# One core, a decode step over a cached K and V: 65 small loads added to the load queue

## The chip, the cores and the metric

The kernel runs on one core of a Trainium2 chip. Its engines are TensorE (PE, matrix products), VectorE (DVE), ScalarE (ACT), GpSimd (POOL) and SyncE (SP). Each runs its own program and waits for the others on semaphores. Data comes from the chip's memory (HBM) into the on-chip buffer of 128 partitions by DMA: an engine, here SP alone, issues a load, and 16 DMA engines carry it out. The metric is the device time of one execution in microseconds (us).

## What is computed

One token for each of two batch rows. x is normalized, projected to 32 heads, and each head attends over 8192 cached keys and values of 128 elements; the result is projected by wo and multiplied by a gate, which is an MLP of the same normalized x. All is 32-bit float.

```python
def ref(x, k_cache, v_cache, wq, wo, w1, b1, w2, b2):   # B=2, H=32, Sk=8192, Dh=128, D=512, F=1376
    xn = layernorm(x)
    q = (xn @ wq).reshape(B, 1, H, Dh).transpose(0, 2, 1, 3)
    scores = einsum("bhqd,bhkd->bhqk", q, k_cache) * Dh ** -0.5
    o = einsum("bhqk,bhkd->bhqd", softmax(scores), v_cache)
    s = o.transpose(0, 2, 1, 3).reshape(B, 1, H * Dh) @ wo
    h = gelu(layernorm(xn) @ w1 + b1) @ w2 + b2
    return x + s * silu(h)
```

## The kernel before

K and V are 256 MB each and are read once. The work is cut into N = 32 iterations, each for one batch row and two heads (U = 2): the K of the two heads lies in one buffer of 128 partitions, 64 for each head, 128 keys of 128 elements in a partition, 64 KB a partition and 8 MB in all. The V of an iteration has the same shape. There are three such buffers: `kb[0]` and `kb[1]` for K in turn, `vb` for V. wq is loaded into `kb[0]` before any K, the small weights w1 and w2 and the values of the MLP lie in `vb` before any V, and wo goes into `vb` after the last V but one. The last V goes into `kb[1]`, in two halves.

In an iteration, DVE multiplies the K buffer by the query in place (`scores_mul`, L524, two halves) and sums over the 128 elements (`scores_sum`, L531). PE and DVE find the largest score (L535 to L541), ACT takes the exponentials (L552), and PE multiplies them with V (`weighted`, L575, 64 matmuls). ACT, PE and DVE then fold that product into a small table Z (L582 to L590). After the last iteration come the division by the sums, the product with wo, in pieces as these land (L650, L659), two DVE operations with the gate (L668, L669), and the store of the result (L670).

All loads go through `load` (L313), which adds one DMA issue to SP's program; SP holds nothing else but waits. A small planner, `Plan`, is told for each operation what it reads and writes, finds which earlier operations it has to wait for, and `emit` writes each engine's program in the order in which the operations were added. Thus SP issues in this order: w1, x, w2, b1, b2, wq, the first K (`load_k(0)`, two halves), the second K (it waits until PE has used wq), the first V, then in turn a K (when DVE has summed the K two before) and a V (when PE has multiplied the V before), the last V, and wo in six pieces (`WO_PIECES`; the last head column in parts of 192 KB and 64 KB). Each load raises a semaphore of the name it is given, by 16 when it is complete; loads on one semaphore are counted together. At the end SP issues the store and waits for it (L125).

PE, DVE and ACT run iterations in a hardware loop; SP's program is written out.

Of the kernel before, what the change touches and what calls it, by code (L numbers as in the profile page):

```python
# [21 lines left out]
class Plan:  # L22
# [18 lines left out]
    def op(self, eng, fn, r=(), w=(), over=(), it=None, loop=False, dma=None):  # L41


        o = Op()
        o.eng, o.fn, o.it, o.loop, o.dma, o.tell = eng, fn, it, loop, dma, False
        need = {}

        def after(d, war):
            if d.dma is None and dma is None and d.eng == eng and (eng == "pe" or war):
                return  # L50
            if d.dma is None:
                if need.get(d.eng) is None or need[d.eng].idx < d.idx:
                    need[d.eng] = d
            else:
                k = ("dma", d.dma)
                if need.get(k) is None or need[k].idx < d.idx:
                    need[k] = d

        for k in r:
            if k in self.writer:  # L60
                after(self.writer[k], False)
        for k in list(w) + list(over):
            if k in self.writer:
                after(self.writer[k], False)
            for d in self.readers.get(k, ()):
                after(d, True)
        clock = self.clock[eng]
        need = {k: d for k, d in need.items() if clock.get(k, 0) < d.idx}
        o.deps = [(k, d) for k, d in need.items()
                  if not any(e is not d and e.done.get(k, 0) >= d.idx for e in need.values())]  # L70
        for _, d in o.deps:
            for k, v in d.done.items():
                clock[k] = max(clock.get(k, 0), v)
        own = eng if dma is None else ("dma", dma)
        self.count[own] = o.idx = self.count.get(own, 0) + 1
        o.done = dict(clock)
        o.done[own] = o.idx
        for k in w:
            self.writer[k] = o
            self.readers[k] = []  # L80
        for k in r:
            if k not in w:
                self.readers.setdefault(k, []).append(o)
        self.ops.append(o)

    def emit(self, heads):

        nc = self.nc
        for o in self.ops:
            for _, d in o.deps:  # L90
                d.tell = True
        sems, value, told = {}, {}, {}
        for o in self.ops:
            key = o.eng if o.dma is None else ("dma", o.dma)
            if key not in sems:
                sems[key] = nc.alloc_semaphore(o.eng if o.dma is None else f"dma_{o.dma}")

            step = 16 if o.dma is not None else int(o.tell or o.eng != "pe")
            told[key] = told.get(key, 0) + step
            value[id(o)] = told[key]  # L100
        for o in self.ops:
            o.waits = {k: value[id(d)] for k, d in o.deps}

        def put(o, waits, turn=None):
            e = self.eng[o.eng]
            for k, v in waits:
                e.wait_ge(sems[k], v)
            i = o.fn() if o.it is None else o.fn(o.it if turn is None else turn)
            if o.dma is not None:
                i.then_inc(sems[("dma", o.dma)], 16)  # L110
            elif o.tell or o.eng != "pe":
                i.then_inc(sems[o.eng], 1)

        def order(d):
            return sorted(d.items(), key=lambda kv: str(kv[0]))

        for e in self.eng:
            ops = [o for o in self.ops if o.eng == e]
            inside = [j for j, o in enumerate(ops) if o.loop]
            if not inside:  # L120
                for o in ops:
                    put(o, order(o.waits))
                if e == "sp":

                    nc.sync.wait_ge(sems[("dma", "out")], told[("dma", "out")])  # L125
                continue
            for o in ops[:inside[0]]:
                put(o, order(o.waits))
            turns = {}
            for j in inside:  # L130
                turns.setdefault(ops[j].it, []).append(ops[j])
            n, m = len(turns), len(turns[1])
            assert inside == list(range(inside[0], inside[-1] + 1)) and list(turns) == list(range(1, n + 1))
            assert all(len(t) == m for t in turns.values())


            body, ahead = [], {}
            for j in range(m):
                col = [turns[i][j] for i in range(1, n + 1)]
                assert len({o.tell for o in col[1:-1]}) == 1, j  # L140
                for o in col:
                    o.tell = col[1].tell
                ws = []
                for k in sorted(set().union(*(o.waits for o in col)), key=str):
                    if all(k not in o.waits for o in col[1:]):
                        ahead[k] = max(ahead.get(k, 0), col[0].waits[k])
                        continue
                    step = col[2].waits[k] - col[1].waits[k]
                    base = col[1].waits[k] - 2 * step
                    for o in col:  # L150
                        assert o.waits.get(k) == step * o.it + base or (o.it == 1 and k not in o.waits), \
                            (e, j, k, o.it, [x.waits.get(k) for x in col])
                    ws.append((k, step, base))
                body.append((col[1], ws))
            for k, v in order(ahead):
                self.eng[e].wait_ge(sems[k], v)
            et = self.eng[e].engine
            with nc.Fori(1, n + 1, 1, engines=bass.OrderedEngineSet([et]), head_slot={et: heads[e]}) as i:
                for o, ws in body:
                    put(o, [(k, i * step + base if base else i * step) for k, step, base in ws], i)  # L160
            for o in ops[inside[-1] + 1:]:
                put(o, order(o.waits))


def decode_kernel(nc, x, kc, vc, wq, wo, w1, b1, w2, b2, out):
    P = 128
# [44 lines left out]
    def sbuf(name, shape):  # L211
        return nc.alloc_sbuf_tensor(name, shape, F32).ap()
# [41 lines left out]
    q_nat = O4  # L254
    rl = sbuf("rl", [P, B])
    on = sbuf("on", [P, RM, OC])


    used = [0]
# [53 lines left out]
    def load(dst, src, sem, w, over=()):  # L313
        op("sp", lambda: nc.sync.dma_start(dst, src), (), w, over=over, dma=sem)  # L314

    def load_k(n):
        i = (n + 1) % 2
        if n in (0, N - 1):
            for s in range(2):
                load(kbuf[i][:, s * M:(s + 1) * M], kf[n][:, s * M:(s + 1) * M], f"k{i}{s}", [("kb", i, s)])  # L320
            return
        load(kbuf[i], kf[n], f"kb{i}", [("kb", i, s) for s in range(2)])
# [10 lines left out]
    for t, src, k in ((b1_sb, b1, "b1"), (b2_sb, b2, "b2")):  # L333
        load(t.rearrange("o (k e) -> o k e", k=16), src.rearrange("(o k e) -> o k e", o=1, k=16), k, [k])
    load(wq_sb, wq.rearrange("(p c) n -> p c n", p=P), "wq", [("kb", 0, s) for s in range(2)])
    load_k(0)


    dve(lambda: nc.vector.memset(eps_t, EPS), w=["eps"])
# [148 lines left out]
    for k in range(N // NB):  # L488

        b, e = divmod(k, HH // NB)  # L490
        i, g = divmod(e, GQ)
# [8 lines left out]

    PT, PM, PN = (t for t in scratch[:3])
    load_k(1)

    def load_v(n):
        load(vbuf, vf[n], "v", ["vb"], over=boot)

    load_v(0)

    def cols(t, a, n):

        return t[:, a:a + n] if isinstance(a, int) else t[:, bass.ds(a, n)]
# [3 lines left out]
    def vector(n, m, fn, r, w):  # L515

        o, e = n % 2, m - n
        dve(lambda i: fn(i * 2 + (e - o)), r, w, it=(n + 1) // 2, loop=0 < n < N - 1)
# [21 lines left out]
    def max_dve(n):  # L540
        vector(n + 1, n, lambda n: nc.vector.tensor_reduce(  # L541
            out=NM, in_=PM[:1, :P].rearrange("o (s r) -> o s r", s=U), axis=AX.X, op=ALU.max, negate=True),
            ["s1"], ["nm"])
# [78 lines left out]
    for i, (a, e) in enumerate(((0, CUT), (CUT, D)), len(WO_PIECES) - 2):  # L622
        load(wo_sb[:, OC - 1, a:e], wo_r[:, OC - 1, a:e], f"wo{i}", [("wo", i)], over=["vb"])

    max_dve(N - 1)
    exps(N - 1)
    weighted(N - 1)
# [72 lines left out]
```

## Time and profile before

| | |
|---|---|
| time, median of 2 runs | 1299.55 us (1299.54 to 1299.55) |
| the profiled execution's own time | 1299.38 us |
| its span, first to last instruction | 1298.1 us |
| busy: DVE, PE, ACT | 1134.3, 408.2, 77.8 us |
| read from HBM | 559.30 MB |

The profile is one execution on the chip, seen by a hardware profiler. Line numbers are those of the kernel. `vb<-in_A_v_cache_dram` is an operation that writes the tile vb from the tensor of the V cache. An engine's name with a q, as in SPq, is its instruction queue, where DMAs are issued. The chain of waits is followed back from the last instruction: at each step to what released it, or to the instruction before it on its engine. The windows view sums, for a stretch of time, each engine's busy time (with the number of instructions), the clock granted to PE, the busy share of the 16 DMA engines and the rate of what they carried; packets are counted where they start, so that over a short stretch the share can pass 1.

### The profile page before, as it was taken

The numbers are of one execution on the slowest core, as the hardware profiler recorded it, in microseconds if no ns is written. First come the engines' busy times: TensorE is split into PE (matmuls) and PEld (weight loads), VectorE is DVE, ScalarE is ACT, GpSimd is POOL, SyncE is SP. The second block draws the span as 40 slices with busy tenths as digits, with TensorE's granted clock in tenths as the row PEclk, the third lists the DMA queues.
The fourth block names the chain that finished last, engine by engine and source line by source line (L and its number), as shares of the span: only waits on it lengthen the run. The fifth ranks groups of instructions, "written<-read, shape, count | busy, mean of one in ns | idle before, by whom it ended". The sixth has DMA issues, their size and how long they took to land.

```text
span 1298.1 us, 6789 instructions
## 1 busy us (share of the span) xinstructions
PE 408.2 (31%) x2728; PEld 123.5 (10%) x2728; DVE 1134.3 (87%) x276; ACT 77.8 (6%) x250; POOL 1.4 (0%) x8
## 2 busy tenths in 40 slices
PE   5603333312333311333321333321333321233337
PEld 1100111000101100101100101000101100001102
DVE  2499999988889988889988888988888988888991
ACT  1200000000000000000000000000000000000000
POOL 0000000000000000000000000000000000000000
PEclk9856666556666556666655666655666655666659
DMA  9999999999999999999999999999999999999998
GB/s 402 449 423 444 428 434 432 426 444 428 436 432 424 446 426 444 428 432 434 426 444 428 434 434 424 446 426 444 426 428 440 426 444 428 434 434 424 433 435 363
DMA packets 11087, 559.45 MB, mean 431 GB/s; under 512 B 1236, under 2 KB 1604, under 8 KB 1736
## 3 DMA queue, kind: packets, MB, share of 16 engines
q1 hardware_dynamic: 11080, 559.36, 99.7%
q8 instruction: 4, 0.07, 0.0%
q14 instruction: 3, 0.02, 0.0%
HBM read 559.30 MB, written 0.06 MB: 431 GB/s over the span
## 4 chain that ended last, share of the span: by engine, by line
DMA 70%; PE 25%; DVE 3%; issue 1%; ACT 0%; SPq 0%; DVEq 0%
DMA vb<-in_A_v_cache_dram 67%; PE po L575 22%; DMA vb<-in_A_wo_dram 2%; DVE kb L524 1%; DVE sc L531 1%; PE s L410 1%; DMA vb<-in_A_x_dram 1%; PE po L482 1%; PE s L452 0%; PE s L412 0%; PE acc L659 0%; DVE vb L418 0%; ACT L431 0%; PE s L459 0%; SPq L314 0%
## 5 line engine op out<-in xcount | busy, mean ns | idle before, releaser
L524 DVE TENSOR_TENSOR kb<-kb,Q 128x8192 f32<-128x8192 f32 x64 | 555.5, 8681 | 102.8 <-DMA kb<-in_A_k_cache_dram 93.5
L531 DVE TENSOR_REDUCE sc<-kb 128x64 f32<-128x8192 f32 x64 | 552.3, 8666 | 0.0
L575 PE MATMUL po<-vb,PZ 128*8 128x512 f32 x1984 | 287.2, 744 | 287.3 <-DMA vb<-in_A_v_cache_dram 286.1
L547 PE MATMUL s<-nm,srow 1*128 1x2 f32 x64 | 18.4, 355 | 361.6 <-DVE nm L541 361.6
L575 PEld LDWEIGHTS po<-vb,PZ 128*8 128x8 f32 x1984 | 57.2, 104 | 491.2 <-issue 487.2
L538 PE MATMUL s<-ident,mx 128*1 128x128 f32 x32 | 11.8, 369 | 191.7 <-DVE mx L535 191.7
L547 PEld LDWEIGHTS s<-nm,srow 1*128 1x128 f32 x64 | 15.7, 302 | 370.9 <-DVE nm L541 370.9
L582 ACT COPY o<-po 128x512 f32<-128x512 f32 x32 | 18.8, 586 | 533.6 <-PE po L575 533.6
L548 ACT COPY bias<-s 128x2 f32<-128x2 f32 x32 | 5.1, 161 | 618.3 <-PE s L547 618.3
L584 PE MATMUL s<-mod,o 128*128 128x2 f32 x256 | 33.6, 253 | 22.1 <-ACT o L582 22.1
L584 PEld LDWEIGHTS s<-mod,o 128*128 128x128 f32 x256 | 31.0, 191 | 51.4 <-ACT o L582 51.4
L552 ACT ACTIVATE PZ<-sc,bias 64x128 f32<-64x128 f32 x64 | 25.5, 399 | 1.8
L538 PEld LDWEIGHTS s<-ident,mx 128*1 128x1 f32 x32 | 2.5, 79 | 195.2 <-DVE mx L535 164.7
L590 DVE TENSOR_TENSOR Z<-blk,s 128x8 f32 (+1 forms) x32 | 5.2, 163 | 12.4 <-PE s L584 12.4
L418 DVE COPY vb<-vb 2x384 f32<-2x384 f32 x4 | 1.8, 501 | 14.5 <-ACT vb L414 14.5
L668 DVE TENSOR_TENSOR gate<-acc,gate 128x128 f32<-128x128 f32 x1 | 0.3, 290 | 13.2 <-PE acc L659 13.2
L552 ACT ACTIVATION_READ_ACCUMULATOR PZ<-sc,bias 64x1 f32 x64 | 11.8, 185 | 0.0
L410 PE MATMUL s<-vb 128*2 128x512 f32 (+1 forms) x24 | 11.1, 610 | 0.3 <-ACT vb L375 0.3
L535 DVE TENSOR_REDUCE mx<-sc 128x1 f32<-128x128 f32 x32 | 9.2, 286 | 1.1
L556 ACT ACTIVATE ZR<-half,rs 128x8 f32 (+1 forms) x32 | 9.6, 302 | 4.1
L575 PE MATMUL po<-kb,PZ 128*8 128x512 f32 x64 | 8.7, 702 | 1.4 <-ACT PZ L552 1.4
L541 DVE TENSOR_REDUCE nm<-s 1x2 f32<-1x128 f32 x32 | 8.7, 272 | 0.3 <-PE s L538 0.3
(88 smaller groups left out, 82.3 us busy)
## 6 DMA issues: line engine op xcount, KB each, us to landing
kb<-in_A_k_cache_dram SPq DMA_DIRECT2D x4, 4096.0 KB, 43.1
kb<-in_A_v_cache_dram SPq DMA_DIRECT2D x2, 4096.0 KB, 40.5
vb<-in_B_w_dram SPq DMA_DIRECT2D x2, 2752.0 KB, 12.0
vb<-in_A_wo_dram SPq DMA_DIRECT2D x1, 4096.0 KB, 20.0
vb<-in_A_wo_dram SPq DMA_DIRECT2D x1, 2048.0 KB, 24.6
vb<-in_A_wo_dram SPq DMA_DIRECT2D x1, 1280.0 KB, 27.2
vb<-in_A_wo_dram SPq DMA_DIRECT2D x1, 512.0 KB, 28.0
vb<-in_A_v_cache_dram SPq DMA_DIRECT2D x31, 29.3
```

What stands on the lines that cost most here:

```text
L410: pe(lambda f=f, w=w, ph=ph, c=c: matmul(ph[:B, :w], yT[:, c, :], w1_sb[:, c, f:f + w], start=(c == 0), stop=False), ["yT", "w1"], [k])
L482: pe(lambda i=i, c=c, wv=wv, a=a, j=j, hd=hd: matmul(PO[R * j:R * j + NQ * B, :].rearrange("m (h d) -> m h d", d=DH), xnT[:, c, a:a + NQ * ...
L524: vector(n, n, lambda n: nc.vector.tensor_tensor(out=k, in0=k, in1=cols(Q, n * DH, DH).unsqueeze(1).to_broadcast([P, M, DH]), op=ALU.mult) ...
L531: vector(n, n, lambda n: nc.vector.tensor_reduce(out=SC[:, s * M:(s + 1) * M], in_=k, axis=AX.X, op=ALU.add), [("kb", i, s)], [("sc", s)])
L535: vector(n, n, lambda n: nc.vector.tensor_reduce(out=MX, in_=SC, axis=AX.X, op=ALU.max), [("sc", 0), ("sc", 1)], ["mx"])
L538: pe(lambda i: transpose(PM[:1, :P], MX, ident), ["mx", "ident"], ["s1"], it=n, loop=n > 0)
L547: pe(lambda i: matmul(PN[:, :U], srow, NM, start=True, stop=True), ["srow", "nm"], ["s2"], **one)
L552: act(lambda i, r=r, s=s: nc.scalar.activation(PZ[r, :, s, :], sc[r], AF.Exp, bias=BIAS[r, s:s + 1], scale=SCALE, accum_out=RS[r]), ["bias ...
L556: act(lambda i: nc.scalar.activation(cols(ZR, i * UP - UP, UP), half, AF.Copy, scale=RS), ["half"] + [("rs", s) for s in range(U)], [("ZR" ...
L575: pe(lambda i, t=t, j=j, v=v: matmul(PO[R * j:R * j + U * JW, :], PZ[:, t].rearrange("p s j -> p (s j)"), v[:, t * JW:(t + 1) * JW, :].rea ...
L582: act(lambda i: nc.scalar.copy(O4, PO), ["po"], ["o4"], **one)
L584: pe(lambda i, k=k: matmul(PT[:, :U], O4[:, k * DH:(k + 1) * DH], mod[:, k:U * JW:JW], start=(k == 0), stop=(k == JW - 1)), ["o4", "mod"], ...
```

## The change

SP's program gets 65 more loads, all on one new semaphore, `mark`. Four groups of 15 (`tags`): the load with n = 15, 14, ... 1 takes the first 8 elements (32 bytes) of n rows of wq to n partitions of a new buffer `marks`. Group 0 stands behind wq, group 1 behind the first K, group 2 behind the first V, group 3 at the end. Ahead of group 3, behind wo, are five loads of 120, 104, 72, 24 and 17 rows of 36 to 40 elements into a new buffer `odd`. No operation reads either buffer. SP's wait at the end is now for `mark` and then for the store.

```diff
                 if e == "sp":
 
-                    nc.sync.wait_ge(sems[("dma", "out")], told[("dma", "out")])
+                    for k in ("mark", "out"):
+                        nc.sync.wait_ge(sems[("dma", k)], told[("dma", k)])
...
+    TAG = 8
+    marks = sbuf("marks", [P, 60 * TAG])
+    odd = sbuf("odd", [P, 5 * 41])
...
+    def tags(i):
+        for n in range(15, 0, -1):
+            load(marks[:n, (15 * i + n - 1) * TAG:(15 * i + n) * TAG], wq[:n, :TAG], "mark", [("mark", i, n)])
+
...
     load(wq_sb, wq.rearrange("(p c) n -> p c n", p=P), "wq", [("kb", 0, s) for s in range(2)])
+    tags(0)
     load_k(0)
+    tags(1)
...
     load_v(0)
+    tags(2)
...
         load(wo_sb[:, OC - 1, a:e], wo_r[:, OC - 1, a:e], f"wo{i}", [("wo", i)], over=["vb"])
+
+    for i, n in enumerate((120, 104, 72, 24, 17)):
+        load(odd[:n, i * 41:i * 41 + 36 + i], wq[:n, :36 + i], "mark", [("odd", n)])
+    tags(3)
 
     max_dve(N - 1)
```

## The prediction

> **What bounds the kernel now.** I read the page first: span, slices, queues, the chain by engine.
>
> ```profile
> span 1298.1 us, 6789 instructions
> ...
> DMA  9999999999999999999999999999999999999998
> GB/s 402 449 423 444 428 434 432 426 444 428 436 432 424 446 426 444 428 432 434 426 444 428 434 434 424 446 426 444 426 428 440 426 444 428 434 434 424 433 435 363
> DMA packets 11087, 559.45 MB, mean 431 GB/s; under 512 B 1236, under 2 KB 1604, under 8 KB 1736
> ...
> q1 hardware_dynamic: 11080, 559.36, 99.7%
> q8 instruction: 4, 0.07, 0.0%
> ...
> DMA 70%; PE 25%; DVE 3%; issue 1%; ACT 0%; SPq 0%; DVEq 0%
> ```
>
> One queue, q1, filled by SP, keeps the 16 DMA engines busy for 99.7% of the span. The busy row is 9 in every slice but the last, so nothing here can finish sooner unless fewer bytes move or they move faster. Next I took the windows view of one whole iteration in the steady part, and the chain in order of time.
>
> ```profile
> core 0: us, PE busy (x) PEld busy (x) DVE busy (x) ACT busy (x) POOL busy (x), PEclk, DMA share, GB/s
> ...
> 200.00:1200.00 1000.00, 292.00 (x1950) 88.05 (x1950) 905.60 (x183) 52.80 (x182) 0.00 (x0) 0.61 1.00 433
> ...
> 1110.00:1148.70 38.70, 11.71 (x87) 3.45 (x79) 35.08 (x8) 2.03 (x7) 0.00 (x0) 0.60 1.00 434
> ```
>
> ```profile
> 1111.12 28.81 DMA vb<-in_A_v_cache_dram
> 1139.93 0.12 issue
> 1140.05 9.19 PE po L575 x64
> ...
> 1266.21 27.20 DMA vb<-in_A_wo_dram
> 1293.41 0.04 issue
> 1293.45 1.28 PE acc L659 x40
> ...
> 1296.11 0.29 DVE gate L669
> ```
>
> An iteration is one K and one V load of 8,388,608 bytes each; the two in 38.70 us are 433.5 GB/s, and the window says 434 with a DMA share of 1.00. The 25% that the chain gives to PE are not a second bound: while PE multiplies one V (1140.05, 9.19 us), the engines carry the next K. The SP rows, with the median time from issue to landing of the K loads, show that the queue does not run dry:
>
> ```profile
> kb<-in_A_k_cache_dram SPq DMA_DIRECT2D x30, 42.6
> ```
>
> ```profile
> start us, us, engine line op out<-in xcount [idle before <-releaser]
> ...
> 1078.01 0.33 SPq L314 DMA_DIRECT2D kb<-in_A_k_cache_dram  x1
> 1111.12 0.33 SPq L314 DMA_DIRECT2D vb<-in_A_v_cache_dram  x1
> 1116.73 0.33 SPq L314 DMA_DIRECT2D kb<-in_A_k_cache_dram  x1
> ...
> 1296.43 0.35 SPq L670 DMA_DIRECT2D out_dram<-gate  x1
> ```
>
> The K issued at 1078.01 lands 42.6 us later by the median of its group, at 1120.6; the V behind it is issued at 1111.12, 9.5 us before that. So what is put into the queue ahead of the last wo bytes is paid in full, and what SP does while it would wait anyway is not.
>
> **The change part by part.** It adds 65 loads to SP: four groups of 15 (a tag, below, is one of these; rows of 32 bytes, 120 rows a group), and five loads of 120 + 104 + 72 + 24 + 17 = 337 rows of 144 to 160 bytes. Nothing is removed, nobody reads the data, and PE, DVE and ACT get no instruction and no wait.
>
> *SP's time.* What SP spends on issuing, and what it waits for, with the start of the program:
>
> ```profile
> L314 SPq DMA_DIRECT2D vb<-in_A_wo_dram x6: 327/428/435, 1265.4 to 1267.9; - x6
> ...
> L314 SPq DMA_DIRECT2D vb<-in_B_b_dram x2: 252/268/283, 1.9 to 2.3; - x2
> ```
>
> ```profile
> 2.56 0.35 SPq L314 DMA_DIRECT2D kb<-in_A_wq_dram  x1
> 2.96 0.94 SPq L314 DMA_DIRECT2D kb<-in_A_k_cache_dram  x2
> ...
> 48.77 0.33 SPq L314 DMA_DIRECT2D kb<-in_A_k_cache_dram  x1
> 49.15 0.43 SPq L314 DMA_DIRECT2D vb<-in_A_v_cache_dram  x1
> 85.74 0.33 SPq L314 DMA_DIRECT2D kb<-in_A_k_cache_dram  x1
> ...
> 1267.53 0.33 SPq L314 DMA_DIRECT2D vb<-in_A_wo_dram  x1
> 1267.91 0.42 SPq L314 DMA_DIRECT2D vb<-in_A_wo_dram  x1
> ```
>
> ```profile
> vb<-in_A_wo_dram SPq DMA_DIRECT2D x1, 192.0 KB, 27.6
> vb<-in_A_wo_dram SPq DMA_DIRECT2D x1, 64.0 KB, 27.4
> out_dram<-gate SPq DMA_DIRECT2D x1, 56.0 KB, 1.6
> ...
> kb<-in_A_wq_dram SPq DMA_DIRECT2D x1, 33.2
> ```
>
> An issue takes 0.25 to 0.44 us, so 15 take 3.8 to 6.6 us. Group 0 stands between wq and the first K: the K issue moves from 2.96 to about 9.5. wq, issued at 2.56, lands at 35.8, so the engines have 26 us of older work: cost 0; without that backlog it would be 6.6. Group 1 then ends near 17, and the next K is held until 48.77 by PE anyway: 0. Group 2 runs from 49.6 to 56.2, and the next K is held until 85.74 by DVE: 0. After wo, issued by 1268.3, come 20 issues, at most 8.8 us, until 1277; SP then has nothing until the out issue at 1296.43: 0, with 19 us of cover.
>
> *Queue time of groups 0 to 2.* This is the only term that reaches the end. No view shows a load of 32-byte rows. The nearest rows are the last two pieces of wo: 128 rows each, 8 an engine. They land at 1267.53 + 27.6 = 1295.13 and 1267.91 + 27.4 = 1295.31, so the last piece, 8 rows of 512 bytes and the completion mark (each load ends in a small write to its semaphore: the page has 1236 packets under 512 bytes), took about 0.18 us, 0.28 with the rounding of the two. That is 0.02 for each of the nine items, of which 512 bytes at 433.5 / 16 = 27.1 GB/s are 0.019 already. A tag on one engine is a row of 32 bytes and a mark: between 0 and 0.04 us, at the very most 0.28. I take 0.02, the middle, since most of the 0.02 an item is bytes that a tag doesn't have. How rows are dealt to the engines no view shows; I count one row of every tag on the same engine, 45 rows and 45 marks: 45 × 0.02 = **0.9 us**. Ends: 0, if that engine is not the one that lands last; 45 × 0.28 = 12.6 at the price of a whole eight-row piece; if all 360 rows and 45 marks lay on one engine, 405 × 0.02 = 8.1. Of the two upper ends I take 8.1 for the range, since 12.6 prices one row as eight. A gain is excluded: no byte less is moved.
>
> The Trainium skill (DMA: Bandwidth & Descriptors, section Why a DMA increments its semaphore by 16 and not by 1) says that a load from SP runs on the lowest-numbered engines, as many as divide its outer dimension. By that page a tag of n rows puts one row on each of the first n engines, the first gets 45 rows, and the sum is the 0.9 above; no view here numbers the engines.
>
> *Queue time behind wo.* The 337 rows and group 3 lie behind the last wo piece, so they hold up only the out load. Spread evenly, 457 rows are 29 an engine, with 20 marks 49 items: 1.0 us, from 1295.3 to 1296.3, just before out is issued at 1296.43: 0. All on one engine, 477 items are 9.5 us, until 1304.8, and out, with 1.6 us of its own, would land at 1306.4 in place of 1298.0: 8.4. I take 0, because an even spread is what 434 GB/s on loads of 128 rows shows.
>
> *The final wait and the code.* The added wait for the marks stands behind the out issue and in front of the wait for out; the marks are in by then.
>
> ```profile
> L125 SPq EVENT_SEMAPHORE  x1: 17/17/17, 1298.0 to 1298.0; - x1
> ```
>
> One more such instruction: 0.02. SP's longer program may need another instruction packet: q8 moves 0.07 MB in 4, some 17 KB each, 0.6 us of one engine at 27.1 GB/s. I take 0 and keep 0.6 for the range.
>
> *Sum.* 0.9 + 0.02 + 0 = 0.9 us. The profiled execution took 1299.38 us, its span of 1298.1 and 1.3 around it; the median of the two runs, 1299.55, is 0.17 above it. On the profile 1300.3, on the median 1300.45; I say 1300.4.
>
> **The rivals.**
>
> *Each tag holds the queue for a small load's whole time* (slower). The out load is issued into an empty queue and takes 1.6 us for 56 KB. If each of the 45 held its engines that long, the stream would be 45 × 1.6 = 72 us late: 1371.6; the 20 behind wo would add up to 32 us before out, less the 1.1 us between 1295.3 and 1296.43: 1402. It decides from 26 / 45 = 0.58 us a tag. For it: 1.6 us is the only row of a small load alone. Against it: the 64 KB piece came 0.18 us behind the one before, so its 1.6 us passed beside other loads. Chance 0.06. The Trainium skill (same page, section Anatomy of one DMA) fits a fixed 2.0 us for each DMA plus its bytes, for loads from another issuer; 45 in a row would be 90 us and 1389.6. It also calls that cost completion latency, with which the 0.18 us agrees.
>
> *The stream's rate changes.* Tags put some engines later than others, and the rest of the stream could run worse or better for it. At 422 GB/s in place of 433 the span would be 1298.1 × 433 / 422 = 1332, so 1333; at 446, 1260, so 1262.
>
> ```profile
> 55.00:90.00 35.00, 1.88 (x9) 0.37 (x5) 34.38 (x6) 1.59 (x3) 0.00 (x0) 0.56 0.97 422
> ```
>
> For it: slices of 424 and of 446 exist. Against it: they alternate and cancel over an iteration (434 in the window), as cuts through long packets would. 0.03 slower, 0.02 faster.
>
> *SP's queue has room for few loads.* The trace has at most 8 or so in flight at the start; now it is 38. If SP were stopped until wq lands at 35.8, the first K would start up to 6.6 us late, and group 1 could do the same to the second K, with 8.8 us for the 20 at the end: up to 22 us, 1321.6, still within 2%. Nothing shows such a stop: the eight issues at the start follow one another. 0.05.
>
> *Nothing at all.* A load is done when its slowest engine is; if another engine than the tags' is last, the delay disappears: 1299.5. 0.22.
>
> **How the numbers follow.** The forecast of about 1 us has 0.58, nothing at all 0.22, the loads piled on one engine 0.04 (1307.6, and 8.4 more with the tail: 1316), the queue's room 0.05, the held queue 0.06, the rate 0.03 and 0.02. The likeliest is 1300.4. The range goes from 1299.2 (no cost, and twice the 0.17 between median and profile) to 1308.2 (8.1 and the 0.6 of code), and leaves out at most 0.20. By 2%, 26 us, about what a measurement of this kernel can tell from no change: slower 0.09, faster 0.02, within 0.89.
>
> **What would show it.** Iterations of 38.7 us at 433 to 434 GB/s as before; V issues after the first ones later by about a microsecond, and by the same amount to the end; the first K issue near 9.5 and the second still near 48.8; 20 issues behind wo by 1277, and out landing about 1.6 us after its issue. The packets under 512 bytes should grow by the 817 rows and the added marks. I am wrong if the delay of the V issues reaches several microseconds already after group 2 (tags that hold the queue), if gaps without DMA appear before 60 us (no room), or if an iteration is longer than 38.7 throughout (the rate).

## The result, and the profile after

| | before | after |
|---|---|---|
| median time | 1299.55 us | 1307.99 us (1307.81 to 1308.16) |
| span of the profiled execution | 1298.1 us | 1306.5 us |

The ratio is 1.0066, with a 95% interval of 1.005 to 1.0083: 8.4 us slower, within 2%. The profiled execution is the one of 1307.81.

First the page of the changed kernel: span, DMA packets, queues, the chain by engine.

```profile
span 1306.5 us, 6854 instructions
...
GB/s 422 398 424 425 437 425 441 419 435 431 435 431 435 431 435 434 433 433 433 435 431 435 431 435 431 435 431 435 429 439 429 437 429 437 429 437 431 433 424 306
DMA packets 12437, 559.52 MB, mean 428 GB/s; under 512 B 2586, under 2 KB 2954, under 8 KB 3086
...
q1 hardware_dynamic: 12430, 559.43, 99.3%
q8 instruction: 4, 0.07, 0.0%
...
DMA 70%; PE 24%; DVE 3%; issue 1%; ACT 0%; another core or an unknown queue 0%; SPq 0%; DVEq 0%
```

The bound is the same, DMA, and 0.07 MB more was moved. Of the 8.4 us that is 0.2. The packets under 512 bytes grew by 1350: the 817 rows that were added and 533 marks (completion writes of 4 bytes). Where the time went is in the chain in order of time (start, duration, what). Before:

```profile
107.40 26.24 DMA vb<-in_A_v_cache_dram
...
142.64 29.71 DMA vb<-in_A_v_cache_dram
...
182.47 28.57 DMA vb<-in_A_v_cache_dram
```

After, the same three V loads, and the end:

```profile
109.38 31.63 DMA vb<-in_A_v_cache_dram
...
150.21 29.50 DMA vb<-in_A_v_cache_dram
...
188.33 30.07 DMA vb<-in_A_v_cache_dram
...
1273.75 26.91 DMA vb<-in_A_wo_dram
1300.66 0.04 issue
...
1303.39 0.29 DVE gate L684
```

The second V of the loop is late by 150.21 - 142.64 = 7.6 us, the third by 5.9, and wo at the end by 1300.66 - 1293.41 = 7.25. So the loss is made in the first 150 us and then only carried along. The windows view (us, busy times, PE clock, DMA share, GB/s) says where in them, and that the rate later is what it was. Before, then after:

```profile
34.00:39.00 5.00, 3.73 (x22) 1.03 (x22) 1.09 (x8) 0.00 (x0) 0.00 (x0) 0.56 0.97 419
...
54.00:61.00 7.00, 2.50 (x12) 0.58 (x8) 7.00 (x2) 2.32 (x4) 0.00 (x0) 0.85 1.05 454
```

```profile
34.00:39.00 5.00, 3.53 (x19) 1.05 (x22) 1.26 (x9) 0.00 (x0) 0.00 (x0) 0.50 0.78 302
...
54.00:61.00 7.00, 3.07 (x16) 0.76 (x12) 7.00 (x2) 2.62 (x5) 0.00 (x0) 0.91 0.97 399
...
1118.66:1157.35 38.69, 11.37 (x75) 3.38 (x75) 35.07 (x8) 2.59 (x8) 0.00 (x0) 0.60 1.00 434
```

Group 0 passes the engines behind wq, from 34.7 on, group 1 behind the first K, from 54.6: there the engines' share falls from 0.97 to 0.78 and from 1.05 to 0.97. Group 2 passes behind the first V, from 93.7 to 99.9. The rest of the 8.4 us is the store: it is issued 7.3 us later than before and lands after 2.7 us instead of 1.6.

```profile
out_dram<-gate SPq DMA_DIRECT2D x1, 56.0 KB, 2.7
```

SP tells a second thing, to which the prediction gave 0.05 (SP's instructions: start, duration with waits):

```profile
3.13 5.48 SPq L318 DMA_DIRECT2D marks<-in_A_wq_dram  x15
8.65 0.83 SPq L318 DMA_DIRECT2D kb<-in_A_k_cache_dram  x2
9.52 26.46 SPq L318 DMA_DIRECT2D marks<-in_A_wq_dram  x15
49.34 0.35 SPq L318 DMA_DIRECT2D kb<-in_A_k_cache_dram  x1
...
50.21 8.61 SPq L318 DMA_DIRECT2D marks<-in_A_wq_dram  x15
...
1275.66 16.89 SPq L318 DMA_DIRECT2D odd<-in_A_wq_dram  x5
1292.59 10.74 SPq L318 DMA_DIRECT2D marks<-in_A_wq_dram  x15
1303.71 0.34 SPq L685 DMA_DIRECT2D out_dram<-gate  x1
```

Group 0 took 5.5 us to issue, as forecast, but group 1 took 26.5, group 2 8.6 and the 20 loads at the end 27.7 instead of 8.8: SP was stopped inside single issues. Two explanations of the loss are thus open: the loads themselves hold an engine, or the full queue does harm.

### The profile page after: what moved, and what is told of

Same layout as the page of the kernel before. It is cut to its first block, busy times and chain, and to the rows that moved or that the text cites. A ratio compares the mean times of both kernels' runs of the same rounds, so it can differ in the third digit from the quotient of the medians.

```text
span 1306.5 us, 6854 instructions
## 1 busy us (share of the span) xinstructions
PE 406.3 (31%) x2728; PEld 123.1 (9%) x2728; DVE 1134.3 (87%) x276; ACT 77.8 (6%) x250; POOL 1.4 (0%) x8
## 4 chain that ended last, share of the span: by engine, by line
DMA 70%; PE 24%; DVE 3%; issue 1%; ACT 0%; another core or an unknown queue 0%; SPq 0%; DVEq 0%
DMA vb<-in_A_v_cache_dram 68%; PE po L586 22%; DMA vb<-in_A_wo_dram 2%; DVE kb L535 1%; DVE sc L542 1%; PE s L420 1%; DMA vb<-in_A_x_dram 1%; PE po L492 1%; PE s L462 0%; PE s L422 0%; PE acc L674 0%; DVE vb L428 0%; ACT L441 0%; SPq L318 0%
## 5 line engine op out<-in xcount | busy, mean ns | idle before, releaser
L586 PE MATMUL po<-vb,PZ 128*8 128x512 f32 x1984 | 284.0, 737 | 300.9 <-DMA vb<-in_A_v_cache_dram 300.9
L601 DVE TENSOR_TENSOR Z<-blk,s 128x8 f32 (+1 forms) x32 | 5.2, 162 | 12.6 <-PE s L595 12.6
## 6 DMA issues: line engine op xcount, KB each, us to landing
vb<-in_A_wo_dram SPq DMA_DIRECT2D x1, 512.0 KB, 27.7
```

What stands on the lines that cost most here:

```text
L586: pe(lambda i, t=t, j=j, v=v: matmul(PO[R * j:R * j + U * JW, :], PZ[:, t].rearrange("p s j -> p (s j)"), v[:, t * JW:(t + 1) * JW, :].rea ...
```

## The experiments

Each changes the kernel after (e10 is written on the kernel before, with its own `marks` and no `odd`); times are medians, and the difference is to the kernel before on the same chip (1299.45, 1299.52 and 1299.62 in the three sets).

| run | what is left or added | time, us | to before | ratio, 95% |
|---|---|---|---|---|
| e1_tail | the five loads and group 3 | 1299.87 | +0.4 | 0.9993 to 1.0013 |
| e2_group2 | group 2 | 1301.15 | +1.7 | 1.0004 to 1.0023 |
| e3_groups01 | groups 0 and 1 | 1304.30 | +4.9 | 1.0023 to 1.0052 |
| e4_one_row | groups 0 to 2, one row a load | 1305.08 | +5.6 | 1.003 to 1.0063 |
| e5_one_load | group 2 as one load | 1300.39 | +0.9 | 0.9997 to 1.0017 |
| e6_each1 | 1 one-row load behind 30 Vs | 1299.51 | 0.0 | 0.9991 to 1.001 |
| e6_each4 | 4 behind 30 Vs | 1300.62 | +1.1 | 1.0 to 1.0019 |
| e7_each8 | 8 behind 30 Vs | 1323.13 | +23.5 | 1.0168 to 1.0205 |
| e6_each15 | 15 behind 30 Vs | 1365.26 | +65.7 | 1.0492 to 1.0537 |
| e8_each15_far | the same, 450 places of wq | 1363.02 | +63.4 | 1.0472 to 1.051 |
| e9_each_one_load | one load of 15 short rows an engine behind 30 Vs | 1311.20 | +11.6 | 1.0071 to 1.0107 |
| e10_each15_3584 | 15 one-row loads of 3584 bytes behind 8 Vs | 1327.63 | +28.0 | 1.0196 to 1.0233 |

### Which of the groups costs

e1_tail takes away groups 0 to 2, e2_group2 all but group 2, e3_groups01 group 2 and the tail:

```diff
# e1_tail
-    tags(0)
     load_k(0)
-    tags(1)
...
     load_v(0)
-    tags(2)
```

> Groups 0 to 2 left out; the five loads of 120 to 17 rows, group 3 and the wait for the marks stay. Theory A (a load's cost falls on the engines of the queue that carry it, 0.13 to 0.2 us a load, and the slowest engine sets the end): only the store's landing is late, 2.7 us in place of 1.6, so +1.1 us on the kernel before. Theory B (the 20 issues keep SP from the store): the store's issue moves behind the gate by several us, +3 or more. If the tail costs nothing, 0.

> Only group 2 is left, the one behind the first V, where SP has 30 us to issue it and the queue has room. Theory A (fixed cost of each load on its engine): 15 x 0.13 = +2.0 us less what slack that engine has, +1 to +2. Theory C (the loss comes only where SP was stopped by a full queue, groups 0 and 1): 15 x 0.012 = +0.2 us.

> Only groups 0 and 1. wo landed 7.25 us later with all three groups. Theory A: two thirds of it or a little more, +5 us. Theory C (full queue alone): all of it, +7 us. Theory D (all engines together pay for the mean work, 22.5 loads of 45): two thirds again, but with engines level.

The tail alone costs 0.4, less than the 1.1 expected; its store landed 1.9 us after its issue. SP's 20 issues did not hold up the store (theory B falls). In e2 SP issued its 15 loads in 5.4 us without a stop, and still 1.7 us were lost, where theory C allows 0.2: a full queue isn't needed. Groups 0 and 1 cost 4.9, as theory A says, 2.4 each on average. The three runs sum to 7.0; the changed kernel lost 8.4. Of the 1.4 between, 0.8 are the store's landing, 2.7 us beside 1.9 in e1: in the changed kernel the last tag's row passes at 1303.94, behind the store's issue at 1303.71, in e1 at 1295.56, a microsecond ahead of it. The other 0.6 stay unexplained.

### Which engine decides

```diff
# e4_one_row (and no loads behind wo)
-            load(marks[:n, (15 * i + n - 1) * TAG:(15 * i + n) * TAG], wq[:n, :TAG], "mark", [("mark", i, n)])
+            load(marks[:1, (15 * i + n - 1) * TAG:(15 * i + n) * TAG], wq[:1, :TAG], "mark", [("mark", i, n)])
```

> Groups 0 to 2 with 15 loads of one row each in place of 15 to 1 rows, no loads behind wo: 45 rows in place of 360. Theory A (slowest engine decides): the same engine carries 45 loads as before, so wo lands as late as in the changed kernel, +6 to +7.5 us. Theory D (mean over engines): 45 / 360 of 7.25, +0.9 us.

An eighth of the rows costs +5.6 us, beside 6.6 for e2 and e3 together. The end of wo in its chain:

```profile
1272.33 27.04 DMA vb<-in_A_wo_dram
1299.37 0.04 issue
```

wo is 5.96 us late. So the mean over the engines (+0.9) is not what counts: one engine that carries a piece of every small load is late, and whoever needs the data waits for it.

### Loads or rows, and how many in a row

```diff
# e5_one_load: group 2 in one load
-        for n in range(15, 0, -1):
-            load(marks[:n, (15 * i + n - 1) * TAG:(15 * i + n) * TAG], wq[:n, :TAG], "mark", [("mark", i, n)])
+        load(marks[:16].rearrange("p (t e) -> p t e", e=2 * TAG)[:, :15, :TAG],
+             wq[:16].rearrange("p (t e) -> p t e", e=2 * TAG)[:, :15, :TAG], "mark", [("mark", i)])
# e6_each4: no groups, no odd loads; e6_each1, e7_each8 and e6_each15 have 1, 8 and 15 in place of 4
+        for n in range(4):
+            s = 4 * i + n
+            a = s // P * TAG
+            load(marks[s % P:s % P + 1, a:a + TAG], wq[:1, :TAG], "mark", [("mark", s)])
...
                 load_v(n)
+                tags(n - 1)
```

> Group 2 as a single load: 16 partitions with 15 pieces of 32 bytes in each, so that each engine gets 15 short rows (240 in place of 120) but one completion mark in place of up to 15. Group 2 alone cost +1.7 us. Theory A1 (the cost belongs to each load and its mark): 0 to +0.3. Theory A2 (it belongs to each short row, whatever load it is in): +1.7 or more.

> Groups 0 to 3 and the five odd loads left out; one load of one row behind each of the 30 V loads that are issued inside the loop, so 30 of them on one engine, never two in a row. Theory A (0.13 us for each load, always): 30 x 0.13 = 3.9 us less a slack of up to 1.3, +2.5 to +4. Theory E (an engine looks a few loads ahead, and a single short load is hidden behind the long packet in front of it): 30 x 0.012 = 0.4 us less the slack, 0.

> The same with four loads of one row behind each of the 30 V loads, 120 in all. Theory A: 120 x 0.13 = 15.6 us less the slack, +14 to +16. Theory E with a lookahead of four loads or more: 120 x 0.012 = 1.4 us, 0 to +1.4; with a lookahead of one or two: between, +4 to +12.

> The same with fifteen loads of one row behind each of the 30 V loads, 450 in all, always on the engine that carries a load of one row. Theory A: 30 x 2.0 = +58 to +62 us on the kernel before, an iteration of 40.7 us in place of 38.7, the other 15 engines waiting. Theory E: as A less the hidden ones, with a lookahead of four 30 x (11 x 0.13 + 15 x 0.012) = +48. Theory F (the loss of about 2 us came once for each group because SP or the queue was upset at the start of the program, and not from the loads themselves): under +10.

> Eight loads of one row of 32 bytes behind each of 30 V loads (the fifteen cost +65.7 us, the four +1.1). Theory E (about four or five loads hidden behind the long packet, each further one about 0.2 us on its engine): 30 x (3 or 4 x 0.2 + 0.1) = +21 to +27. Theory G (a step: once the queue of short loads is long enough the whole loss of about 1.8 us appears): +55 to +60, or again about +2.

e5 lies between its two theories, and its interval reaches both. The row of e6 and e7 is plain: 0.0, 1.1, 23.5, 65.7 us for 1, 4, 8 and 15 loads behind each V. By group that is 0, 0.04, 0.78 and 2.19 us. From 8 to 15 each load costs (2.19 - 0.78) / 7 = 0.20 us, and the line meets zero at 8 - 0.78 / 0.20 = 4. So about four small loads in a row are free, and each one behind them holds its engine for 0.2 us on average. A constant price (theory A) fails at 1 and at 4, a single step (G) at 8. The windows of e6_each4 in the first fence, of e6_each15 in the second:

```profile
700.00:820.00 120.00, 33.83 (x225) 10.18 (x225) 108.88 (x22) 6.08 (x21) 0.00 (x0) 0.60 1.01 435
```

```profile
160.00:240.00 80.00, 20.82 (x150) 6.57 (x150) 72.58 (x15) 4.06 (x14) 0.00 (x0) 0.63 1.00 432
700.00:820.00 120.00, 33.56 (x225) 10.14 (x225) 102.76 (x22) 6.09 (x21) 0.00 (x0) 0.61 0.97 411
```

With fifteen, the first iterations still run at 432 GB/s, which fits that the other 15 engines have loads queued and run ahead. Later the rate is 411: they have caught up with what SP can release, and wait for the late one. SP is not stopped inside its issues here; each fifteen took it 4.4 to 4.9 us:

```profile
713.47 0.35 SPq L318 DMA_DIRECT2D vb<-in_A_v_cache_dram  x1
713.87 4.50 SPq L318 DMA_DIRECT2D marks<-in_A_wq_dram  x15
```

The chain of e6_each15 shows the longer iteration, 631.61 to 672.64 and on to 713.47, 41.0 and 40.8 us, on average 2.2 more than 38.7:

```profile
631.61 31.86 DMA vb<-in_A_v_cache_dram
...
672.64 31.54 DMA vb<-in_A_v_cache_dram
...
713.47 31.57 DMA vb<-in_A_v_cache_dram
```

The packet records of the same trace show how the engine spends it (start in us + duration in ns: bytes; 32 is a row, 4 a mark; the middle left out):

```
703.793+9:4  703.799+9:32  703.805+9:4  703.811+9:32  703.817+9:4  703.822+9:32
...
703.946+9:4  703.952+9:32  703.958+9:4  703.964+9:32  703.970+9:4  703.975+4215:65536
```

The fifteen rows and marks pass in 0.18 us, 0.012 a load, less than I had forecast. It is the long packet behind them that takes 4215 ns in place of 2418: 1.8 us are lost there. The same packet takes over 4.2 us in 24 of the 30 groups, and behind the eight loads of e7 3.0 to 3.2 us in 27 of 30. In e6_each4, from 120 us on, one packet of 64 KB is over 200 ns longer than 2418 (by 415 ns), and none by more. In e2 the loss stands between the small rows, as idle engines: its 120 rows, 7 to 9 ns each, begin between 93.0 and 95.9 us.

### Other reasons: the place read, the rows, the bytes

```diff
# e8_each15_far, against e6_each15
-            load(marks[s % P:s % P + 1, a:a + TAG], wq[:1, :TAG], "mark", [("mark", s)])
+            load(marks[s % P:s % P + 1, a:a + TAG], wq[s:s + 1, TAG * n:TAG * n + TAG], "mark", [("mark", s)])
# e9_each_one_load, against e6_each15
+        load(marks[16 * (i % 8):16 * (i % 8) + 16, i // 8 * 15 * TAG:(i // 8 + 1) * 15 * TAG].rearrange("p (t e) -> p t e", e=TAG),
+             wq[:16].rearrange("p (t e) -> p t e", e=2 * TAG)[:, :15, :TAG], "mark", [("mark", i)])
# e10_each15_3584, against e6_each15
-    TAG = 8
+    TAG = 896
... (marks has one column of TAG, odd is gone; each row goes to marks[s:s + 1])
-        for n in range(15):
+        for n in range(15 if i < 8 else 0):
```

> Fifteen loads of one row behind each of 30 V loads, but each from another row and column of wq instead of 450 times the same 32 bytes. Theory A or E (cost of a load as such): +66 as before, within 3. Theory H (all loads read the same bytes of HBM, and reads of one place wait for each other): well under that, +5 to +30.

> One load of 16 partitions with 15 pieces of 32 bytes each behind each of 30 V loads: 15 short rows and one mark on every engine. Once, it cost +0.9 us. If rows cost as loads do, +60 or more; if a row in one load costs about half of a load (a row without its own mark), 30 x 0.9 = +27; if only marks cost, 30 x 0.1 = +3.

> Fifteen loads of one row of 3584 bytes behind each of the first 8 V loads of the loop, 120 in all. By bytes alone a row is 0.132 us at 27.1 GB/s, 15 rows with marks 2.07 us, 8 groups 16.6. Fifteen rows of 32 bytes cost 2.19 us a group, 17.5 for 8. Theory I (the fixed time of a load passes beside its bytes; the longer of the two counts): +16 to +19. Theory J (fixed time and bytes add up): +30 to +34.

Reading 450 places instead of one makes no difference worth naming (H falls). Fifteen rows in one load cost 0.39 us a group where fifteen loads cost 2.19: what costs is the load, not the row. Whether it is the load itself or its mark isn't separated, and all the small loads raise one semaphore, `mark`; no run gives them several. e5, the same done once, cost 0.9, more than the 0.39; the difference is about what a run scatters and isn't explained.

e10 lost 28.0 / 8 = 3.5 us a group, between I (2.1) and J (4.0). The packet records of the first group show rows 0.14 us apart up to the sixth, which is their bytes, and from there on 0.26 to 0.32 apart (its first eight rows; marks left out):

```
132.328+145:3584  132.475+140:3584  132.617+140:3584  132.760+140:3584  132.902+140:3584  133.044+256:3584  133.303+284:3584  133.589+322:3584
```

5 × 0.14 + 10 × 0.3 = 3.7, near the 3.5. This is the slowest of the eight groups; the rows of the others take 2.8 to 3.2 us, and the long packet behind them up to 0.4 longer than 2418 ns. So the fixed time comes on top of the bytes at least in part (J more than I), and mostly from the fifth or sixth load on.

## Why the prediction was right, and where it wasn't

**Direction and size.** Within 2% was forecast and came; 1307.99 lies in the range, 0.2 below its end. That it does is luck: the forecast value, +0.9, was a ninth of the truth, and the end of the range came from a case that did not happen, all rows on one engine at 0.02 us each. What happened is 45 loads on one engine at 0.16 each on average. One of the prediction's own signs of being wrong came too: the V issues are late by 7.6 us soon after group 2, where it had said about a microsecond.

**The term that was mis-sized.** The step is the price of a tag: "0.02, the middle", between 0 and 0.04. wo's delay of 7.25 us over 45 tags is 0.16. By the experiments' own price three groups of fifteen make 3 × 2.19 = 6.6. I had taken the price from the last piece of wo, which landed 0.18 us behind the one before it. That was one small load behind larger ones, nearest to e6_each1, where it is free. No row of the trace before had more than a few small loads in a row, so it could show the price of the first, not of the fifteenth. The end that I thought too high, 0.28 a tag (12.6 us), was about as far from 0.16 as the one I took.

**The rule on which engine.** That a load from SP takes the lowest-numbered engines, as many as divide its outer dimension (the Trainium skill, DMA: Bandwidth & Descriptors, section Why a DMA increments its semaphore by 16 and not by 1), agrees with e4 and e6_each15: 450 one-row loads, to 128 different partitions, delayed one engine by the sum of all, 65.7 us; spread over 16 engines they could have cost a sixteenth or less. My count of 45 on one engine stands. The marks agree too. Of the 533, 480 are one for each row of the tags, and 53 are left for the five loads of 120, 104, 72, 24 and 17 rows, whose largest divisors up to 16, 15 + 13 + 12 + 12 + 1, sum to 53. By this the 17 rows lay on one engine (in e1 they pass within 0.17 us), so the even spread that the prediction took behind wo was not what came.

**The held queue.** This rival, 0.06, had the right mechanism and the wrong price: a fixed time for each load, 0.2 us from the fifth on, not the 1.6 of the store. The 2.0 us for each DMA that the Trainium skill fits for loads from another issuer (same page, section Anatomy of one DMA) is not what these loads held their engine for: fifteen in a row took 2.19 together.

**SP's queue room.** Right that there is a limit, which I gave 0.05: single issues took up to 7.9 us (one of the five loads behind wo). No price of it is shown: e2 lost 1.7 us and e6_each15 2.19 a group without a stop. Groups 0 and 1 lost 4.9 together, with stops in group 1 alone, so at most 4.9 - 2 × 1.7 = 1.5 us could be its doing. The cover named in the prediction held, for the second K (49.34, 0.6 late) as for the store. For the store the cover was nearly used up: SP finished issuing at 1303.33, and the gate was ready at 1303.68.

**The rest.** The rate is 434 GB/s after as before, so that rival is out. The instruction packets of q8 are 4 before and after: nothing for code. The first K was issued at 8.65, forecast 9.5. For the loads behind wo I took 0; the store landed 1.1 us later after its issue; alone, in e1, these loads cost 0.4.

## What to carry to other kernels

Price a small load by the engine that carries it and by how many stand in a row, not by its bytes: here four in a row behind a long load were free and each further one held its engine for 0.2 us, whatever the other 15 did. The one-row loads all fell on the same engine, so their times added up; put such data in one load, or place the loads singly behind long ones. And a price read from one operation in a trace is the price of one: ask whether the row shows the case that the change makes.

## What the runs showed of the hardware that was not expected

SP's issues stopped, and the lengths of the stops suggest that a queue was full and SP waited for whole packets to leave it. Three issues of group 1 in a row:

```profile
13.76 4.33 SPq L318 DMA_DIRECT2D marks<-in_A_wq_dram  x1
...
18.13 4.79 SPq L318 DMA_DIRECT2D marks<-in_A_wq_dram  x1
...
22.96 7.20 SPq L318 DMA_DIRECT2D marks<-in_A_wq_dram  x1
```

4.79 and 7.20 are near two and three times the 2.42 us of a 64 KB packet of wq. A count of what had been issued and not yet carried at 13.76 on the engine that gets a row of every load: 2 or 3 packets of w2, 8 of wq and 16 of the first K, 21 small rows, b1 and b2, with the marks some 75. That is one reading of one place, not a measured limit. What within an engine costs the 0.2 us, and why only from the fifth load on, no run here tells.
